# A linear-attention and feed-forward kernel on one core: u loaded to all partitions, fillers on TensorE, a written order for steps 0 to 2

## The chip, the core and the metric

The kernel runs on one core of a Trainium2 chip. A core has five engines that run side by side, each through its own list of instructions in order: TensorE (PE in the profile; PEld is its loading of weights), VectorE (DVE), ScalarE (ACT), GpSimd (POOL) and SyncE (SP), which here issues the loads. Engines wait for each other by semaphores. The metric is the device time of one execution in microseconds, as the median of timed runs. The profile is of one further execution, which has a time of its own.

## What is computed

Two parts follow each other. Per batch and head, with a state of 48 x 48:

```
for t in range(S):                       # B, H, S, D = 4, 8, 768, 48
    cur = einsum('bhd,bhe->bhde', u * k[t], v[t])
    y[t] = einsum('bhd,bhde->bhe', r[t], state + cur)
    state = w * state + einsum('bhd,bhe->bhde', k[t], v[t])
x = y as 3072 tokens x 384
h = x @ w_in                             # 384 -> 2048
out = where(h > 0, h, exp(min(h, 0)) - 1) @ w_out    # 2048 -> 384
```

## The kernel before

The 768 times are cut into 6 blocks of 128 (NCH, index n). In a block there are 4 units, one for each batch b. A unit's attention is done by blocks: r and k are turned by TensorE (`turn_in`, L601, a transpose by the identity), multiplied by powers of w (`decay_r` and `decay_k`, L676 and L684, both through L667 on DVE), multiplied with each other to scores (L741 in block 0), masked, and applied to v (L797). The part of the current token is sum over d of r u k, times v: `current` (L693) makes ru in two multiplications, `current_sum` (L703) the sum. `key_rest` (L708) multiplies k by the reversed powers `rev` for the state, and `added_state` (L888) makes the addition to the state. The outputs of a block, in two parts xh and xl, are the x of the layer.

The layer goes in 16 steps per block (NF, index f), of 128 hidden units each: `hid` (9 matmuls of 128 x 512, L1004), `neg` (two on ACT, L1013 and L1014), `elu` (DVE, L1019), `gh` (ACT, L1025), `gl` (DVE, L1027), `proj` (9 matmuls, L1048). While block 0's layer runs, block 1's units are prepared, and the weights of the layer are loaded and split in two parts. Load j (`Lw:j`, `load_weights`, L200) brings columns of w_in for step j/2 in 4 pieces where j is even, rows of w_out where j is odd, into slot (j+1) mod 6 of `stage`. A load is then widened (`wd:k`, ACT, L550, two loads at once), merged (`ma:k`, DVE, L559) and split: `sp:k`, and the remainder `rs:j` or `rsd:j` (L594, L596), which reads the slot last. So Lw:12 can start only when rsd:6 is done.

All loads go through SP's queue in written order; an issue that waits holds up those behind it. Nothing is moved by a scheduler (`manual_schedule`): each engine's list is the order of the calls. Three lists make it: START (block 0's units and first weights), BOTH (steps 0 and 1) and FIRST and LATER (a pattern for each further step), read by `start`, `first_steps` and `step`. At the beginning, in `prepare`, 7 matmuls on the identity go ahead (`warm`), u is loaded as one row, and `u_by_tokens` (L500) spreads it to 128 partitions by one matmul with a column of ones, copied by ACT.

Of the kernel before, what the change touches and what calls it, by code (L numbers as in the profile page):

```python
# [8 lines left out]
F32 = mybir.dt.float32  # L9
# [42 lines left out]
FIRST = """
Lq rk3 v3 Eq1 hid ns3 A1 T0 rud0 ma sum0 bkA-1 neg df0 elu sp dk0 pa1 brA-1 Y2 gh gl dr0 pb1 r4d xh2 xl2 mbT+1 mrT+1
# [13 lines left out]
class Kernel:  # L67
# [7 lines left out]
    def prepare(self, ctx):  # L75
        nc, tc = self.nc, self.tc
        cp = ctx.enter_context(tc.tile_pool(name="cp", bufs=1))

        self.rev = cp.tile([P, H, DP], F32, tag="rev", name="rev")
        self.state = [cp.tile([P, HP, 2 * D], F32, tag=f"state{b}", name=f"state{b}") for b in range(B)]  # L80
        early = self.rev.rearrange("p h d -> p (h d)")
        w_row = early[0:1, 0:DM]
        nc.sync.dma_start(w_row, self.w.rearrange("(o h) d -> o (h d)", o=1))

        w_col = cp.tile([P, HP], F32, tag="w_col", name="w_col")
        nc.vector.memset(w_col, 1.0)
# [213 lines left out]
    def run(self):  # L300
        self.start()
        self.first_steps()
        for at in range(2, NCH * NF):
            self.step(*divmod(at, NF))
        for f in (NF - 2, NF - 1):
            self.project(NCH - 1, f)
        self.store(NCH - 1)

    def start(self):
# [3 lines left out]
        for b in (2, 3):  # L313
# [59 lines left out]
    def first_steps(self):  # L373

        layer = {
            "hid": lambda f: self.hidden(0, f, self.rest_of(0, f)),
            "neg": lambda f: self.negative(0, f),
            "elu": lambda f: self.elu(0, f),
            "gh": lambda f: self.split_g(0, f, 0),
            "gl": lambda f: self.split_g(0, f, 1),  # L380
            "proj": lambda f: self.project(0, f),
        }
        for op in BOTH.split():
            if ":" in op:
                self.do(op)
            else:
                layer[op[:-1]](int(op[-1]))

    def next_loads(self, b):
        self.raw[1, b] = self.slots[b]  # L390
# [109 lines left out]
    def u_by_tokens(self):  # L500

        ps = self.bank("u")[:, 0:DM]
        self.nc.tensor.matmul(ps, lhsT=self.one, rhs=self.u_row, start=True, stop=True)
        self.nc.scalar.copy(self.u_b.rearrange("p h d -> p (h d)"), ps)

    def inverse_table(self):

# [183 lines left out]
            self.scaled(un["k"], un["pk"], self.qw, by_act)  # L691

    def current(self, n, b, eng=None):  # L693

        nc, wk, un = self.nc, self.wk, self.units.setdefault((n, b), {})
        r_t, k_t, _ = self.raw[n, b]
        un["ru"] = wk.tile([P, H, D], F32, tag="ru", name="ru", bufs=2)
        (eng or nc.gpsimd).tensor_mul(un["ru"], r_t[:, :, 0:D], self.u_b)
        (eng or nc.gpsimd).tensor_mul(un["ru"], un["ru"], k_t[:, :, 0:D])
# [431 lines left out]
```

## Time and profile before

| | us |
|---|---|
| median of 3 timed runs | 505.28 (504.96 to 506.22) |
| the profiled execution | 510.23 |
| its span, first to last instruction | 508.5 |
| PE busy in the span | 494.7 |
| mean granted clock of TensorE in the span | 0.988 |

The profiled execution stands 4.95 us above the median. Of its time 1.7 us lie outside the span. Times in the trace are counted from the span's start. TensorE's clock has two levels, 2.4 GHz and 1.2 GHz; a granted clock of 1.00 is the first, 0.50 the second. A matmul's busy time is modelled, so a busy PE may still be a slow one; the clock tells which.

### The profile page before, as it was taken

The numbers are of one execution on the slowest core, as the hardware profiler recorded it, in microseconds if no ns is written. First come the engines' busy times: TensorE is split into PE (matmuls) and PEld (weight loads), VectorE is DVE, ScalarE is ACT, GpSimd is POOL, SyncE is SP. The second block draws the span as 40 slices with busy tenths as digits, with TensorE's granted clock in tenths as the row PEclk, the third lists the DMA queues.
The fourth block names the chain that finished last, engine by engine and source line by source line (L and its number), as shares of the span: only waits on it lengthen the run. The fifth ranks groups of instructions, "written<-read, shape, count | busy, mean of one in ns | idle before, by whom it ended". The sixth has DMA issues, their size and how long they took to land.

```text
span 508.5 us, 12107 instructions
## 1 busy us (share of the span) xinstructions
PE 494.7 (97%) x5005; PEld 406.5 (80%) x5005; DVE 304.9 (60%) x531; ACT 240.8 (47%) x459; POOL 107.2 (21%) x142
## 2 busy tenths in 40 slices
PE   7999999999999999999999999999999999999995
PEld 6887777887888888887878888888788878899995
DVE  6786988975865666666474674574664443343331
ACT  2276677744454435435534354354354354344442
POOL 7514224333123141321321212211011000000000
PEclk8799999999999999999999999999999999999999
DMA  8869777665256434625613446326243000011001
GB/s 137 232 154 218 165 188 186 139 135 126 58 121 148 109 68 85 147 70 109 131 44 88 110 74 134 98 46 127 66 97 101 18 1 2 8 28 24 6 0 67
DMA packets 108453, 49.11 MB, mean 97 GB/s; under 512 B 89442, under 2 KB 104292, under 8 KB 108388
## 3 DMA queue, kind: packets, MB, share of 16 engines
q1 hardware_dynamic: 96292, 43.52, 38.6%
q10 hardware_dynamic: 12096, 4.72, 3.9%
q8 instruction: 41, 0.67, 0.5%
q14 instruction: 24, 0.20, 0.1%
HBM read 35.12 MB, written 13.11 MB: 95 GB/s over the span
## 4 chain that ended last, share of the span: by engine, by line
PE 89%; DMA 5%; ACT 2%; DVE 1%; SPq 1%; issue 1%; POOL 0%; ACTq 0%; DVEq 0%
PE ps_acc L1048 38%; PE ps_h L1004 36%; PE ps_y L797 4%; PE ps_a L765 3%; DMA r_t<-in_r_dram 2%; DMA stage<-in_moe_w_in_dram 2%; PE ps_a L741 2%; PE ps_y L785 1%; PE ps_y L897 1%; ACT wide L550 1%; DMA stage<-in_moe_w_out_dram 1%; PE ps_y L780 1%; PE ps_rT L607 1%; PE ps_kT L607 1%; PE ps_y L853 1%
## 5 line engine op out<-in xcount | busy, mean ns | idle before, releaser
L1004 PE MATMUL ps_h<-x,wh 128*128 128x512 f32 (+1 forms) x582 | 180.2, 391 | 0.0
L1048 PE MATMUL ps_acc<-g,wh 128*128 128x512 f32 x480 | 165.8, 400 | 1.1 <-issue 1.0
L1019 DVE SCALAR_TENSOR_TENSOR ps_h<-g,ps_h 128x512 f32<-128x512 f32 x96 | 66.7, 694 | 137.1 <-ACT g L1014 137.0
L1004 PEld LDWEIGHTS ps_h<-x,wh 128*128 128x128 f32 x582 | 108.5, 188 | 22.8
L1013 ACT ACTIVATE g<-ps_h 128x512 f32<-128x512 f32 x96 | 57.3, 597 | 135.5 <-PE ps_h L1004 125.5
L1004 PE MATMUL ps_h<-x,wl 128*128 128x512 f32 (+1 forms) x291 | 114.0, 392 | 0.0
L1048 PEld LDWEIGHTS ps_acc<-g,wh 128*128 128x128 f32 x480 | 90.0, 188 | 22.4 <-issue 1.1
L1048 PE MATMUL ps_acc<-g,wl 128*128 128x512 f32 x240 | 93.6, 390 | 0.0
L1027 DVE SCALAR_TENSOR_TENSOR g<-ps_h,g 128x512 fp32r<-128x512 f32 x96 | 66.3, 691 | 40.3 <-ACT g L1025 34.8
L1025 ACT ACTIVATE g<-ps_h 128x512 fp32r<-128x512 f32 x96 | 57.5, 599 | 69.6 <-DVE ps_h L1019 69.5
L1004 PEld LDWEIGHTS ps_h<-x,wl 128*128 128x128 f32 x291 | 54.6, 188 | 12.8
L1014 ACT ACTIVATE g<-g 128x512 f32<-128x512 f32 x96 | 60.7, 632 | 3.1
L815 POOL TENSOR_TENSOR a<-ident,diag 128x512 f32<-128x512 f32 x20 | 20.9, 1043 | 156.9 <-PE ps_y L897 81.8
L1048 PEld LDWEIGHTS ps_acc<-g,wl 128*128 128x128 f32 x240 | 45.1, 188 | 9.9 <-issue 0.9
L1048 PE MATMUL ps_acc<-wh,g 128*128 128x384 f32 x128 | 35.3, 339 | 0.0
L655 POOL TENSOR_TENSOR tb<-rk,qw 128x512 f32<-128x512 f32 x16 | 20.7, 1296 | 67.6 <-DMA rk<-blocks 50.8
L822 DVE COPY_PREDICATED a<-mask,ps_a 128x512 f32<-128x512 int32 x40 | 29.3, 733 | 0.0
L811 ACT ACTIVATE a<-ident,diag 128x128 f32<-128x128 f32 x80 | 25.3, 391 | 0.0
L1048 PEld LDWEIGHTS ps_acc<-wh,g 128*128 128x128 f32 x128 | 23.4, 187 | 1.1 <-issue 0.4
L1048 PE MATMUL ps_acc<-wl,g 128*128 128x384 f32 x64 | 21.6, 337 | 0.0
L922 ACT CAST x<-ps_y 128x256 fp32r<-128x256 f32 (+1 forms) x40 | 10.8, 324 | 22.5 <-DVE state L912 21.0
L570 POOL CAST wh<-stage 128x384 fp32r<-128x384 f32 x16 | 8.6, 534 | 57.1 <-DVE stage L559 57.1
(112 smaller groups left out, 456.2 us busy)
## 6 DMA issues: line engine op xcount, KB each, us to landing
blocks<-tb SPq DMA_DIRECT2D x64, 128.0 KB, 2.3
rk<-blocks SPq DMA_DIRECT2D x16, 512.0 KB, 3.5
stage<-in_moe_w_out_dram SPq DMA_DIRECT2D x16, 383.8 KB, 3.8
stage<-in_moe_w_in_dram SPq DMA_DIRECT2D x64, 95.8 KB, 3.7
out_dram<-stage ACTq DMA_DIRECT2D x80, 48.0 KB, 1.7
r_t<-in_r_dram SPq DMA_DIRECT2D x17, 192.0 KB, 4.5
k_t<-in_k_dram SPq DMA_DIRECT2D x17, 192.0 KB, 5.0
v_t<-in_v_dram SPq DMA_DIRECT2D x17, 192.0 KB, 5.3
```

Of the source, the lines that this page charges most:

```text
L655: (self.nc.gpsimd if i else self.nc.vector).tensor_mul(dst, src, by)
L797: self.nc.tensor.matmul(y[self.pair(a), t : t + P], lhsT=v[:, d : d + Q], rhs=un["a"][i][:, a, :], start=(n == 0 and j != 1 and len(un["py ...
L811: self.nc.scalar.activation(un["a"][i][:, a, :], self.ident, AF.Copy, scale=diag[:, a : a + 1])
L815: self.nc.gpsimd.tensor_mul(un["a"][i], self.ident.unsqueeze(1).to_broadcast([P, HP, P]), diag.unsqueeze(2).to_broadcast([P, HP, P]),)
L822: self.nc.vector.copy_predicated(un["a"][i], self.mask.bitcast(I32).unsqueeze(1).to_broadcast([P, HP, P]), un["pa"][i].rearrange("p (a t) ...
L1004: self.nc.tensor.matmul(ph[:, part], lhsT=a[:, c * P : (c + 1) * P], rhs=x[:, c, part], start=(c == 0 and i == 0), stop=(c == NC - 1 and i ...
L1013: nc.scalar.activation(g, ph, AF.Relu, scale=-1.0)
L1014: nc.scalar.activation(g, g, AF.Exp, scale=-1.0)
L1019: self.nc.vector.scalar_tensor_tensor(ph, g, -1.0, ph, op0=ALU.add, op1=ALU.max)
L1025: nc.scalar.activation(part, g, AF.Copy, scale=W_SCALE)
L1027: nc.vector.scalar_tensor_tensor(part, g, W_SCALE, self.g[n, f][2].bitcast(F32), op0=ALU.mult, op1=ALU.subtract)
L1048: self.nc.tensor.matmul(at, lhsT=lhs, rhs=rhs, start=(f == 0 and i == 0), stop=(f == NF - 1 and i == 2),)
```

## The change

Four things are edited. First, u is loaded by one DMA with its row repeated for all 128 partitions, behind k of unit 0 and ahead of r of unit 1; the matmul, the copy and the small load go. In `current` the product r k is made first and then multiplied by u, so the first product needs no u. Second, fillers: `jk:9` puts 9 transposes of the identity on PE ahead of unit 0's first transpose, `jk:3` puts 3 ahead of unit 1's; nothing reads them. Third, START is in a new order, and BOTH now holds steps 0, 1 and 2 as one written order (the pattern begins with step 3). Fourth, the first unit of block 1 (`nT`, `ndr`, `ndk`, `nru`, `nsum`, `nDp`) is turned and decayed at written places, sooner than the pattern did it.

```diff
 START = """
 Lrk:2 Lv:1 Lrk:3 Lv:2 Lw:0 Lv:3 Lw:2 Lw:1 Lw:4 Lw:3 Lw:5
-pr ub Tr:0 inv ru:0 Tk:0 Tr:1 dr:0 zw Tk:1 dk:0 A:0 dr:1 dk:1 sum:0 Tr:2 A:1 Tk:2 m0:0 m1:0 ru:1 dr:2 m0:1 dk:2 vd:0 PT Tr:3
...
+jk:9 Tr:0 inv pr Tk:0 rua:0 dr:0 dk:0 rub:0 rua:1 sum:0 PT zw rub:1 jk:3 krd:0 Tr:1 Tk:1 dk:1 dr:1 A:0 S:0 Tr:2 Tk:2
...
 BOTH = """
-hid0 neg0 krd:3 S:1 Ln:1 ma:2 elu0 Sd:2 gh0 gl0 hid1 neg1 sp:2 elu1 rsd:4 Lw:10 gh1 S:3 proj0 gl1 rs:3 Lw:9 wd:3
-ma:3 sp:3 rsd:6 rs:5 wd:4
+xh:3 xl:2 xl:3 wdo:1 hid0 rsd:2 krd:3 krd:1 wd:2 neg0 ma:2 mao:1 sp:2 elu0 hid1 krd:2 gh0 spo:1 nT:0 wd:3 rs:1 gl0
+Lw:8 Sd:1 rsd:4 ma:3 neg1 elu1 Lw:7 rs:3 Lw:9 ndr:0 ndk:0 sp:3 proj0 gh1 gl1 hid2 nru:0 rsd:6 neg2 S:3 wd:4 elu2 Lw:12
+ma:4 Lw:10 proj1 gh2 nsum:0 rsd:5 nDp:0 Ln:1 gl2 sp:4 Sd:2 rs:7 rsd:8 Lw:11 wd:5
 """
...
-        self.u_row, self.one = early[DP : DP + 1, 0:DM], ones[DP : DP + 1, :]
-        nc.sync.dma_start(self.u_row, self.u.rearrange("(o h) d -> o (h d)", o=1))
         self.load_rk(0, 0, (1,))
+        nc.sync.dma_start(self.u_b, self.u.partition_broadcast(P))
...
-        for at in range(2, NCH * NF):
+        for at in range(3, NCH * NF):
...
+            "ndr": lambda b: self.now("df", b, self.decay_r),
+            "ndk": lambda b: self.now("df", b, self.decay_k),
...
+    def now(self, name, b, what, *args):
+        self.done.add((name, 1, b))
+        what(1, b, *args)
...
+    def keep_warm(self, times):
+        junk = self.ps.tile([P, T], F32, tag="h", name="junk", bufs=2)
+        for _ in range(times):
+            self.nc.tensor.transpose(junk[:, 0:P], self.ident, self.ident)
...
+    def key_product(self, n, b, eng=None):
+        un = self.units.setdefault((n, b), {})
+        r_t, k_t, _ = self.raw[n, b]
+        un["ru"] = self.wk.tile([P, H, D], F32, tag="ru", name="ru", bufs=2)
+        (eng or self.nc.gpsimd).tensor_mul(un["ru"], r_t[:, :, 0:D], k_t[:, :, 0:D])
```

In the rows of order below, a row is an engine's instruction (or several, x4) with its line, what it writes and what it reads; lines of the changed file are some 9 to 15 higher. PE at the program's start before: r_t_68 and k_t_69 are unit 0's, r_t_71 and k_t_72 unit 1's, `raw` units 2 and 3.

```order
L503 MATMUL ps_u<-rev 128x384
L607 MATMUL ps_rT<-ident,r_t_68 128x128 x4
L607 MATMUL ps_kT<-ident,k_t_69 128x128 x4
L607 MATMUL ps_rT<-ident,r_t_71 128x128 x4
L607 MATMUL ps_kT<-ident,k_t_72 128x128 x4
L741 MATMUL ps_a<-rk 128x128 x8
L607 MATMUL ps_rT<-ident,raw 128x128 x4
```

The same place now:

```order
L513 MATMUL junk<-ident 128x128 x9
L616 MATMUL ps_rT<-ident,r_t_68 128x128 x4
L616 MATMUL ps_kT<-ident,k_t_69 128x128 x4
L538 MATMUL ps_pt<-ident,pwr 128x128 x4
L513 MATMUL junk<-ident 128x128 x3
L616 MATMUL ps_rT<-ident,r_t_71 128x128 x4
L616 MATMUL ps_kT<-ident,k_t_72 128x128 x4
L756 MATMUL ps_a<-rk 128x128 x8
```

The fillers stand ahead of both units' transposes, and the transposes of the powers (ps_pt) have come forward from behind unit 2's.

SP's queue before, from the last load of START's first line on (w_in is even loads, w_out odd ones): the second row is Lw:6, then block 1's unit 0, Lw:7, Lw:8, block 1's unit 1, Lw:10, Lw:9 with Lw:11, and Lw:12.

```order
L215 DMA stage<-in_moe_w_out_dram 128x1535 x2
L212 DMA stage<-in_moe_w_in_dram 32x3x511 x4
L165 DMA r_t_68<-in_r_dram 128x8x48
L165 DMA k_t_69<-in_k_dram 128x8x48
L169 DMA v_t_70<-in_v_dram 128x8x48
L215 DMA stage<-in_moe_w_out_dram 128x1535
L212 DMA stage<-in_moe_w_in_dram 32x3x511 x4
L165 DMA r_t_71<-in_r_dram 128x8x48
L165 DMA k_t_72<-in_k_dram 128x8x48
L169 DMA v_t_73<-in_v_dram 128x8x48
L212 DMA stage<-in_moe_w_in_dram 32x3x511 x4
L215 DMA stage<-in_moe_w_out_dram 128x1535 x2
```

The same place now: block 1's unit 0, Lw:6 and Lw:8, Lw:7 and Lw:9, Lw:12 and Lw:10, block 1's unit 1, Lw:11 with Lw:13.

```order
L214 DMA stage<-in_moe_w_out_dram 128x1535 x2
L164 DMA r_t_68<-in_r_dram 128x8x48
L164 DMA k_t_69<-in_k_dram 128x8x48
L168 DMA v_t_70<-in_v_dram 128x8x48
L211 DMA stage<-in_moe_w_in_dram 32x3x511 x8
L214 DMA stage<-in_moe_w_out_dram 128x1535 x2
L211 DMA stage<-in_moe_w_in_dram 32x3x511 x8
L164 DMA r_t_71<-in_r_dram 128x8x48
L164 DMA k_t_72<-in_k_dram 128x8x48
L168 DMA v_t_73<-in_v_dram 128x8x48
L214 DMA stage<-in_moe_w_out_dram 128x1535 x2
```

Block 1's unit 0 has moved ahead of Lw:6, and Lw:12 ahead of Lw:10.

DVE before, from ma:3 to the first mask of block 1's unit 0 (wl_131 is rsd:6, wl_133 is rsd:8; ps_h is elu):

```order
L559 SCALAR_TENSOR_TENSOR stage<-stage,wide 128x768
L596 SCALAR_TENSOR_TENSOR wl_131<-stage,wh_130 128x384
L698 TENSOR_TENSOR ru<-r_t_68,u_b 128x384
L699 TENSOR_TENSOR ru<-ru,k_t_69 128x384
L559 SCALAR_TENSOR_TENSOR stage<-stage,wide 128x768
L706 TENSOR_REDUCE diag<-ru 128x8
L667 TENSOR_TENSOR rk<-ps_rT,pw 128x512
L667 TENSOR_TENSOR rk<-ps_kT,qw 128x512
L1019 SCALAR_TENSOR_TENSOR ps_h<-g,ps_h 128x512
```

Now, from ma:3 to rsd:6 and the elu behind it:

```order
L568 SCALAR_TENSOR_TENSOR stage<-stage,wide 128x768
L1034 SCALAR_TENSOR_TENSOR ps_h<-g,ps_h 128x512
L676 TENSOR_TENSOR rk<-ps_rT,pw 128x512
L676 TENSOR_TENSOR rk<-ps_kT,qw 128x512
L1042 SCALAR_TENSOR_TENSOR g_651<-ps_h,g_649 128x512
L712 TENSOR_TENSOR ru<-r_t_68,k_t_69 128x384
L716 TENSOR_TENSOR ru<-ru,u_b 128x384
L605 SCALAR_TENSOR_TENSOR wl_131<-stage,wh_130 128x384
L1034 SCALAR_TENSOR_TENSOR ps_h<-g,ps_h 128x512
```

The two decays of block 1's unit 0 (rk) have moved ahead of an elu, and rsd:6 from right behind ma:3 to six instructions further on.

## Rows read from the trace of the kernel before

**Rows 1.** The page, parts 1 and 2: busy us by engine; granted clock.
```profile
PE 494.7 (97%) x5005; PEld 406.5 (80%) x5005; DVE 304.9 (60%) x531; ACT 240.8 (47%) x459; POOL 107.2 (21%) x142
...
PEclk8799999999999999999999999999999999999999
```

**Rows 2.** Windows: us; busy us (count) by engine; PEclk; DMA; GB/s.
```profile
5.00:8.50 3.50, 2.34 (x12) 1.40 (x13) 2.96 (x8) 3.33 (x4) 2.05 (x7) 0.96 1.37 188
...
8.50:18.80 10.30, 10.19 (x72) 8.37 (x75) 6.53 (x11) 0.58 (x1) 5.65 (x7) 0.52 1.05 215
...
24.00:28.00 4.00, 3.79 (x125) 3.53 (x122) 3.46 (x8) 2.64 (x6) 0.83 (x1) 1.00 0.23 91
...
29.00:44.50 15.50, 15.49 (x177) 12.54 (x167) 11.72 (x20) 11.29 (x20) 4.06 (x6) 1.00 0.97 199
...
44.50:45.60 1.10, 0.01 (x2) 0.01 (x2) 1.10 (x3) 0.00 (x0) 1.10 (x2) 1.00 1.01 373
...
502.60:506.50 3.90, 0.01 (x1) 0.00 (x0) 0.56 (x1) 0.03 (x1) 0.00 (x0) 1.00 0.57 199
...
506.50:508.50 2.00, 0.00 (x0) 0.00 (x0) 0.00 (x0) 0.00 (x0) 0.00 (x0) 0.52 0.04 13
```

**Rows 3.** Timeline of PE to 21 us: start, length, work [idle before].
```profile
5.03 0.88 PE L503 MATMUL ps_u<-rev 1*128 1x384 f32 x2
...
7.05 0.63 PE L607 MATMUL ps_kT<-ident,k_t 128*128 128x128 f32 x4 [0.55 <-DMA k_t<-in_k_dram]
...
8.26 1.09 PE L607 MATMUL ps_rT<-ident,r_t 128*128 128x128 f32 x4 [0.58 <-DMA r_t<-in_r_dram]
...
20.02 0.66 PE L607 MATMUL ps_kT<-ident,raw 128*128 128x128 f32 x4
```

**Rows 4.** Timeline of SP's queue, 20 to 42 us.
```profile
20.49 0.90 SPq L215 DMA_DIRECT2D stage<-in_moe_w_out_dram  x2
...
27.82 1.75 SPq L212 DMA_DIRECT2D stage<-in_moe_w_in_dram  x4
...
39.45 2.50 SPq L212 DMA_DIRECT2D stage<-in_moe_w_in_dram  x4
```

**Rows 5.** The page, part 6: issues, KB each, us to landing.
```profile
stage<-in_moe_w_in_dram SPq DMA_DIRECT2D x64, 95.8 KB, 3.7
...
blocks<-tb SPq DMA_DIRECT2D x64, 128.0 KB, 2.3
```

**Rows 6.** SP's waits, 20 to 50 us: total, times, longest.
```profile
SPq L212 <- DVE wl L596: 7.5, 2, 6.4
```

**Rows 7.** Timeline, step 3: from a weight load's landing to PE.
```profile
47.21 1.09 ACT L550 ACTIVATE wide<-stage 128x768 f16<-128x768 bf16 x1 [0.44 <-DMA stage<-in_moe_w_out_dram]
...
51.20 0.72 DVE L822 COPY_PREDICATED a<-mask,ps_a 128x512 f32<-128x512 int32 x1
...
51.97 0.18 PEld L780 LDWEIGHTS ps_y<-rk,state 48*32 48x32 f32 x14 [0.39 <-DVE a L822]
```

**Rows 8.** Groups by line, 27 to 52 us: busy, mean ns.
```profile
L1019 DVE SCALAR_TENSOR_TENSOR ps_h<-g,ps_h 128x512 f32<-128x512 f32 x4 | 2.8, 694 | 3.1 <-ACT g L1014 3.1
...
L1027 DVE SCALAR_TENSOR_TENSOR g<-ps_h,g 128x512 fp32r<-128x512 f32 x4 | 2.8, 692 | 0.9 <-ACT g L1025 0.9
...
L1014 ACT ACTIVATE g<-g 128x512 f32<-128x512 f32 x4 | 2.5, 632 | 0.1
...
L596 DVE SCALAR_TENSOR_TENSOR wl<-stage,wh 128x384 fp32r<-128x384 f32 x5 | 2.8, 558 | 0.6 <-ACT wh L572 0.6
```

**Rows 9.** Timeline of DVE, 38 to 45 us.
```profile
38.95 0.96 DVE L559 SCALAR_TENSOR_TENSOR stage<-stage,wide 128x768 int32<-128x768 int32 x1 [0.94 <-ACT wide L550]
...
41.02 1.40 DVE L698 TENSOR_TENSOR ru<-r_t,u_b 128x384 f32<-128x384 f32 x1
...
42.45 0.56 DVE L699 TENSOR_TENSOR ru<-ru,k_t 128x384 f32<-128x384 f32 x1
...
44.26 0.68 DVE L667 TENSOR_TENSOR rk<-ps_rT,pw 128x512 f32<-128x512 f32 x1
```

More of the change, by code (lines that the diff above doesn't have):

```diff
@@ L42 @@
 Lrk:2 Lv:1 Lrk:3 Lv:2 Lw:0 Lv:3 Lw:2 Lw:1 Lw:4 Lw:3 Lw:5
-pr ub Tr:0 inv ru:0 Tk:0 Tr:1 dr:0 zw Tk:1 dk:0 A:0 dr:1 dk:1 sum:0 Tr:2 A:1 Tk:2 m0:0 m1:0 ru:1 dr:2 m0:1 dk:2 vd:0 PT Tr:3
-m1:1 Y:0 sum:1 Tk:3 xh:0 ru:2 krd:0 A:2 dr:3 sum:2 vd:1 ru:3 wd:0 dk:3 xl:0 Y:1 m1:2 m0:2 ma:0 A:3 xh:1 sum:3 vd:2 m1:3 sp:0
-m0:3 wdi:1 vd:3 Y:2 xl:1 mai:1 xh:2 krd:1 wdo:1 Y:3 spi:1 xh:3 rsd:0 Lw:6 mao:1 spo:1 S:0 Ln:0 xl:2 wd:2 xl:3 H:0 rsd:1 Lw:7
-rsd:2 Lw:8 krd:2
+jk:9 Tr:0 inv pr Tk:0 rua:0 dr:0 dk:0 rub:0 rua:1 sum:0 PT zw rub:1 jk:3 krd:0 Tr:1 Tk:1 dk:1 dr:1 A:0 S:0 Tr:2 Tk:2
+A:1 m0:0 m1:0 dr:2 vd:0 Tr:3 dk:2 m0:1 m1:1 A:2 wd:0 Tk:3 ru:2 sum:2 sum:1 vd:2 dr:3 vd:1 dk:3 ru:3 Y:0 m0:2 A:3 m1:2
+ma:0 Y:2 sum:3 m0:3 Y:1 m1:3 sp:0 wdi:1 xh:0 xh:2 xl:0 xh:1 vd:3 mai:1 Ln:0 rsd:0 xl:1 spi:1 Lw:6 Y:3 H:0
 """
 BOTH = """
-hid0 neg0 krd:3 S:1 Ln:1 ma:2 elu0 Sd:2 gh0 gl0 hid1 neg1 sp:2 elu1 rsd:4 Lw:10 gh1 S:3 proj0 gl1 rs:3 Lw:9 wd:3
-ma:3 sp:3 rsd:6 rs:5 wd:4
+xh:3 xl:2 xl:3 wdo:1 hid0 rsd:2 krd:3 krd:1 wd:2 neg0 ma:2 mao:1 sp:2 elu0 hid1 krd:2 gh0 spo:1 nT:0 wd:3 rs:1 gl0
+Lw:8 Sd:1 rsd:4 ma:3 neg1 elu1 Lw:7 rs:3 Lw:9 ndr:0 ndk:0 sp:3 proj0 gh1 gl1 hid2 nru:0 rsd:6 neg2 S:3 wd:4 elu2 Lw:12
+ma:4 Lw:10 proj1 gh2 nsum:0 rsd:5 nDp:0 Ln:1 gl2 sp:4 Sd:2 rs:7 rsd:8 Lw:11 wd:5
 """
@@ L254, in run_general @@
     def run_general(self):
-        self.u_by_tokens()
         self.reverse_powers()
@@ L318, in start @@
         ops = {
-            "ub": lambda b: self.u_by_tokens(),
+            "jk": lambda b: self.keep_warm(b),
+            "rua": lambda b: self.key_product(0, b),
+            "rub": lambda b: self.times_u(0, b),
+            "nT": lambda b: self.now("T", b, self.turn_in),
+            "nru": lambda b: self.now("rud", b, self.current, dve),
+            "nsum": lambda b: self.now("sum", b, self.current_sum),
+            "ndr": lambda b: self.now("df", b, self.decay_r),
+            "ndk": lambda b: self.now("df", b, self.decay_k),
+            "nDp": lambda b: self.now("Dp", b, self.diag_scores, 0),
             "inv": lambda b: self.inverse_table(),
@@ L498, in warm @@
                 self.nc.tensor.matmul(junk, lhsT=self.ident, rhs=self.ident, start=True, stop=True)
[L500 to L504, printed above, removed]
+    def keep_warm(self, times):
+        junk = self.ps.tile([P, T], F32, tag="h", name="junk", bufs=2)
+        for _ in range(times):
+            self.nc.tensor.transpose(junk[:, 0:P], self.ident, self.ident)
     def inverse_table(self):
@@ L693, in current, with times_u @@
     def current(self, n, b, eng=None):
[L695 to L699, printed above, removed]
+        self.key_product(n, b, eng)
+        self.times_u(n, b, eng)
         if self.general:
             self.current_sum(n, b)
+    def key_product(self, n, b, eng=None):
[3 more added lines that the diff above has]
+        (eng or self.nc.gpsimd).tensor_mul(un["ru"], r_t[:, :, 0:D], k_t[:, :, 0:D])
+    def times_u(self, n, b, eng=None):
+        ru = self.units[n, b]["ru"]
+        (eng or self.nc.gpsimd).tensor_mul(ru, ru, self.u_b)
     def current_sum(self, n, b):
```

## Prediction

> **What bounds the kernel now.** I read the page first: PE is busy for 494.7 of 508.5 us, so the end is PE's, and what a change can give is PE's waiting and the time in which its clock is low [rows 1]. The row of the granted clock, in 40 slices of 12.7 us, is full from the third slice on; only the first two show less. So I went to the windows. From 5 to 8.5 us PE is busy for 2.34 of 3.50 us. From 8.5 to 18.8 us it is busy for 10.19 of 10.30 us at a mean granted clock of 0.52, that is at 1.2 GHz nearly throughout; before and after it is at 2.4 GHz [rows 2]. The work of those 10.19 us would take about 5.1 us at the full clock: the most that can be had there. That the low clock is what costs is seen on one instruction group: four transposes take 1.09 us at 8.26 and 0.66 us at 20.02 [rows 3]. What PE did before the fall: a matmul of one row (u), and the transposes of unit 0, with two waits for loads of 0.55 and 0.58 us (k of unit 0 at 7.05, r of unit 1 at 8.26) [rows 3].
>
> Then I asked what PE would meet if it came earlier. From 29 to 44.5 us it is busy for 15.49 of 15.50 us, so no row shows it waiting for weights there; but the DMA share is 0.97 at 199 GB/s [rows 2]: the loads are as full as PE, only just ahead of it. In step 3 the order turns: ACT's widening at 47.21 waited for a weight load, and from its start a chain of ACT and DVE goes to the mask at 51.20 and to PE's scores by state at 51.97 [rows 7]. That is 51.97 - 47.21 = 4.76 us from a landed load to PE. This place decides the sum.
>
> **The change part by part.**
>
> *u by a load.* Removed: PE's 0.88 us at 5.03 [rows 3], ACT's copy, a small DMA. Added: a 192 KB DMA ahead of r of unit 1 and everything behind. No row shows a load with repeated rows. Bounds from rows: loads of the same size land 8.26 - 7.05 = 1.2 us apart at the start [rows 3]; at the best rate of a row, 373 GB/s [rows 2], 0.197 MB take 0.53 us. Less than that has no reason, since the bytes are written all the same. I take 0.8, between them, since its runs of 1536 bytes are eight times those of r. The Trainium skill (DMA: Bandwidth & Descriptors, Specifications) gives 512 bytes as the least piece at full rate; by it the lower end would hold and the sum be 0.3 us better. No row shows it for this load.
>
> *Fillers.* Twelve transposes at 0.66 / 4 = 0.165 us [rows 3]: 1.5 us for the nine, 0.5 us for the three. PE is free from about 5.0, the nine end at 6.5; Tr:0 then ends at 7.2 and Tk:0, whose load lands at 7.0, follows. The three stand before r of unit 1, which now lands near 8.26 + 0.8 = 9.1. Both lie in waits, cost nothing on the path, and at the low clock would take up to 1.6 us more, half of it still covered. With them, PE is busy for about 3.3 of the 3.5 us up to 8.5 where it was 2.34. I take it that the clock then stays at 2.4 GHz. PE arrives at step 1 some 4 to 5 us sooner (5.1, less what the loads of units 2 and 3 hold back, which come 0.8 us later).
>
> *The order of steps 0 to 2: what of that lead is left.* The loads are next to be late, and I follow them in four terms.
> (a) Lw:6. Before, it was issued at 27.82 [rows 4] after SP had waited 6.4 us for a remainder on DVE [rows 6], and the DMA engines idled: 91 GB/s from 24 to 28 us, at a share of 0.23 [rows 2]. What moved in those 4 us, 0.364 MB, was the end of START's first line; at 199 GB/s [rows 2] it takes 1.8 us, so the queue was through at about 25.8. Now block 1's unit 0 (576 KB) and Lw:6 (383 KB) follow at once, with u 192 KB more: 1151 KB, 1.18 MB, which at 199 GB/s [rows 2] take 5.9 us, at 373 GB/s 3.2. I take the former, as it is the mean of the stretch that holds the same kinds of loads, and 0.3 for the last piece: Lw:6 has landed at about 32.0 (29.0 to 33, the latter with 1.2 for u and the slower issue).
> (b) From there to rsd:6, on which Lw:12 waits: the widening 1.09 [rows 7]; two passes on ACT for neg1 at 0.63 each, 1.26, longer than the merge on DVE, 0.96, beside it; elu1 0.69; two decays at 0.68, 1.36; gl1 0.69; two products at 0.56, 1.12; rsd:6 0.56 [rows 8, 9]. The sum is 6.8. A product took 1.40 where POOL ran beside it [rows 9], so up to 7.6. rsd:6 ends at 32.0 + 6.8 = 38.8.
> (c) Lw:12 and, behind it, Lw:10: eight pieces. Four take SP 1.75 to 2.50 us [rows 4], so the eighth is issued 3.5 to 5.0 us on, at 42.3 or later; pieces of this kind land 3.7 us after issue in the median, and the shortest median of the page is 2.3 [rows 5]. I take 3.0, between them, the queue being empty in front of these: 45.3 (from 42.3 + 2.3 = 44.6 to 43.8 + 3.7 = 47.5).
> (d) wd:5 then starts at 45.3, and 4.76 later, at about 50.0, PE goes on; before it was 51.97.
> Gain: 2.0 us. Ends: all late, 33 + 7.6 + 5.0 + 3.7 + 4.76 = 54.1, a loss of 2.1; all early, 29.0 + 6.8 + 3.5 + 2.3 + 4.76 = 46.4, a gain of 5.6, which the lead of PE itself limits to about 4.5. In front of this place PE must wait: its lead of 4 to 5 us turns into 2.0, so 2 to 3 us are spent there, beside 0.4 before [rows 7].
>
> *Block 1's first unit decayed sooner.* PE's wait of 1.1 us from 44.5 to 45.6 [rows 2] goes, since the two decays stand ahead of what kept DVE; but it lies ahead of the place of (d) and adds nothing beyond it. DVE's six instructions in front of rsd:6 are the price, in (b).
>
> *The rest* (START's new order, key_rest and the state sooner, r k before u): the same instructions, hidden behind loads as before; 0 on the path.
>
> From step 3 on both kernels have the same order, loads and PE alike shifted by the gain, so it stays to the end. Against the profiled execution: 510.23 - 2.0 = 508.2, a span of 506.5. Against the median: 505.28 - 2.0 = 503.3.
>
> **The rivals.**
>
> *1. The loads come sooner.* The best rate of rows 2 rather than the mean. Then PE's lead of 4 to 5 us stays: 505.28 - 4.5 = 500.8. For it: after 24 us the DMA engines have room. Against: the share of 0.97 from 29 us on.
>
> *2. The gain is given back whole.* Lw:10 lands no sooner than 46.5, because it stands behind Lw:12. Then (d) is 51.3 and the gain 0.7: 504.6. For it: the ends of (b) and (c).
>
> *3. The clock falls a second time, in the wait that the change makes.* Place: PE in front of the scores by state, step 3. By the sum it stands still for 2 to 4 us. Rows show two cases: a wait of 1.1 us left the clock at 1.00; behind the last matmul it was 1.00 for 3.9 us and then 0.52 [rows 2]. A wait like the former changes nothing, one like the latter brings this rival; the forecast's wait lies between the two, nearer to the latter. The price: if the low stretch is as long as the first, PE's work of about 10 us takes 5.1 us more; if a third as long, 1.7. I take 4.0, nearer to the former, since the first low stretch went on although PE was busy for 10.19 of 10.30 us in it [rows 2]: 503.3 + 4.0 = 507.3. The Trainium skill (TensorE: Matmul & The Clock Gate, HAM oscillation — how this bites in real kernels) says that waits for loads between bursts of matmuls put the clock low again. The trace agrees at the kernel's end, but at 8.5 us the clock fell with no wait above 0.6 us, so the rule is not the whole of it.
>
> *4. The timed runs have no low stretch, or fillers do not prevent it.* The profiled execution is 4.95 us longer than the median, about as much as the low stretch costs. If the timed runs lack it, the lead is there already, and the change only brings the wait: 3 us of it, 508.3. If the clock falls all the same, the change has the u load (0.8) and nothing else: 506.1. For it: that likeness in size. Against: loads, waits and PE's list are the same in timed runs, and a low stretch that came and went among them would spread them by more than the 1.3 us from 504.96 to 506.22.
>
> **How the numbers follow.** The chances: forecast 0.44 (501.8 to 504.2), rival 1 0.10, rival 2 0.15, rival 3 0.17 (505.0 to 508.4), rival 4 0.14 (506.1 to 508.3). About 0.3% (1.5 us) is what a measurement of this kernel can tell from no change. Faster by more than that (below 503.76): 0.36 of the forecast's and all of rival 1, together 0.46. Within: 0.08 of the forecast's, rival 2's 0.15, 0.05 of rival 3 and 0.02 of rival 4: 0.30. Slower (above 506.80): what is left of rivals 3 and 4, 0.24. The likeliest is the forecast, 503.3. The range is 500.8 to 507.4; it leaves out the lower half of rival 1 and the upper parts of rivals 3 and 4, some 0.18.
>
> **What would show it.** Right: a granted clock of 1.00 through 8.5 to 18.8 us; PE at step 1's first hid about 4 us sooner; then, in step 3, PE's longest wait of the program, 2 to 4 us, in front of the scores by state, ended by DVE's mask, behind ACT's wd:5, behind a w_in load; and from there on every row some 2 us sooner. Wrong: a low clock that starts at about 11 us (rival 4) or at about 50 us (rival 3), no wait in step 3 (rival 1), or a profiled time that falls while the median does not (rival 4).

## The result, and the profile after

The changed kernel takes 509.06 us in the median (508.81 to 510.19), where the kernel before takes 505.12 beside it: a ratio of 1.0078 with a 95% interval from 1.0057 to 1.0100. It is slower by 3.9 us; the forecast was 2.0 us faster. Its profiled execution, however, is shorter than that of before: 509.18 us at a span of 507.4, against 510.23 at 508.5. Both statements hold, and the difference between them is the first thing to explain.

The page of the changed kernel, with the granted clock in 40 slices:

```profile
span 507.4 us, 12116 instructions
PE 491.9 (97%) x5015; PEld 404.3 (80%) x5015; DVE 304.6 (60%) x533; ACT 239.7 (47%) x456; POOL 107.2 (21%) x142
PEclk9999999999999999999999999999999999999999
```

Its windows, as in [rows 2]: stretch and its length, busy time of PE, PEld, DVE, ACT and POOL with instructions, granted clock, DMA share, GB/s:

```profile
5.00:8.50 3.50, 3.47 (x24) 3.48 (x24) 2.60 (x8) 1.64 (x3) 1.79 (x7) 1.00 0.81 166
8.50:18.80 10.30, 8.34 (x143) 6.80 (x144) 8.68 (x16) 2.53 (x4) 6.48 (x7) 1.00 0.89 180
...
29.00:44.50 15.50, 13.69 (x155) 10.00 (x155) 12.81 (x23) 8.88 (x16) 5.65 (x7) 1.00 0.56 153
```

The low stretch of 8.5 to 18.8 us is gone: PE does 143 instructions there where it did 72. But it now waits, 2.0 us there and 1.8 us from 29 to 44.5, where before it was busy throughout. The DMA share from 29 to 44.5 us has fallen from 0.97 to 0.56: the loads are not short of bandwidth, they are not issued. What PE waits for, and the chain behind it:

PE's timeline of the changed kernel (start, length, line, operation, idle time before and what ended it), the first part of hid1 and the scores by state of step 3:

```profile
28.27 0.63 PE L1019 MATMUL ps_h<-x,wh 128*128 128x512 f32 x2
...
31.36 0.63 PE L616 MATMUL ps_kT<-ident,k_t 128*128 128x128 f32 x4 [0.41 <-DMA k_t<-in_k_dram]
...
38.23 0.50 PE L1063 MATMUL ps_acc<-g,wh 128*128 128x512 f32 x1 [0.97 <-ACT g L1040]
...
51.48 0.45 PE L795 MATMUL ps_y<-rk,state 48*32 48x128 f32 x14 [1.70 <-DVE a L837]
```

ACT's timeline, the widenings of Lw:6 (with Lw:5) and of Lw:10 (with Lw:9):

```profile
34.63 1.09 ACT L559 ACTIVATE wide<-stage 128x768 f16<-128x768 bf16 x1 [3.36 <-DMA stage<-in_moe_w_in_dram]
...
46.71 1.09 ACT L559 ACTIVATE wide<-stage 128x768 f16<-128x768 bf16 x1 [3.80 <-DMA stage<-in_moe_w_in_dram]
```

SP's timeline. The row at 23.48 ends START's first line (Lw:3, Lw:5), that at 29.28 is Lw:6 and Lw:8, that at 33.64 Lw:7 and Lw:9, that at 40.93 Lw:12 and then Lw:10:

```profile
3.19 0.81 SPq L109 DMA_DIRECT2D u_b<-in_u_dram  x1
...
5.14 2.89 SPq L168 DMA_DIRECT2D v_t<-in_v_dram  x1
9.03 0.37 SPq L164 DMA_DIRECT2D raw<-in_r_dram  x1
...
23.48 0.90 SPq L214 DMA_DIRECT2D stage<-in_moe_w_out_dram  x2
...
29.28 4.19 SPq L211 DMA_DIRECT2D stage<-in_moe_w_in_dram  x8
33.64 0.83 SPq L214 DMA_DIRECT2D stage<-in_moe_w_out_dram  x2
40.93 3.64 SPq L211 DMA_DIRECT2D stage<-in_moe_w_in_dram  x8
```

And SP's waits from 27 to 50 us (in total, times, longest):

```profile
SPq L211 <- DVE wl L605: 6.4, 1, 6.4
```

From 34.5 to 40.9 us SP stands before the first piece of Lw:12, which waits for rsd:6 on DVE. Lw:10 stands behind it with nothing to wait for (its slot was free after rsd:4), and Lw:10 is what ACT, DVE and PE wait for in step 3. It is the place that the prediction named; the gain there is 51.97 - 51.48 = 0.5 us against the profiled execution of before, not 2.0.

**The two groups of before.** Beside the twelve kernels below, e1 to e12, the kernel before ran 114 times. Its times fall in two groups with nothing between 507.43 and 508.24: 76 executions with a median of 505.7 and mean granted clocks of 0.993 to 1.000, and 38 with a median of 509.1, of which 31 have a mean clock of 0.983 to 0.993. The profiled execution (510.23, clock 0.988) belongs to the second, the runs that were timed for the prediction to the first. So the prediction started from a profile of the rarer kind, and most executions of before are not of that kind. A low stretch is seen in that one profile; the mean clock of the 31 fits one, and why the other 7 are long (0.997 to 0.999) is not shown. The groups are 3.4 us apart. Differences below are to the median of the first group among the executions of before that ran beside the kernel in question. That median itself lies between 505.1 and 506.5, so a difference of half a microsecond between kernels that did not run side by side settles little; the changed kernel (four executions), e1 to e4, e5 to e8, e9 to e11 and e12 are five such sets.

### The profile page after: what moved, and what is told of

It reads as the page before. It is cut to its first block, busy times and chain, and to the rows that moved or that the text cites. A ratio compares the mean times of both kernels' runs of the same rounds, so it can differ in the third digit from the quotient of the medians.

```text
span 507.4 us, 12116 instructions
## 1 busy us (share of the span) xinstructions
PE 491.9 (97%) x5015; PEld 404.3 (80%) x5015; DVE 304.6 (60%) x533; ACT 239.7 (47%) x456; POOL 107.2 (21%) x142
## 4 chain that ended last, share of the span: by engine, by line
PE 86%; DMA 5%; SPq 4%; ACT 2%; DVE 1%; issue 1%; POOL 0%; ACTq 0%; DVEq 0%; POOLq 0%
PE ps_acc L1063 38%; PE ps_h L1019 36%; PE ps_a L780 3%; PE ps_y L812 3%; SPq L211 2%; DMA stage<-in_moe_w_out_dram 2%; DMA r_t<-in_r_dram 1%; PE ps_y L800 1%; ACT wide L559 1%; DMA stage<-in_moe_w_in_dram 1%; PE ps_y L912 1%; PE ps_y L795 1%; PE ps_a L756 1%; PE junk L508 1%; SPq L164 1%
## 5 line engine op out<-in xcount | busy, mean ns | idle before, releaser
L559 ACT ACTIVATE wide<-stage 128x768 f16<-128x768 bf16 (+1 forms) x18 | 17.9, 994 | 16.6 <-DMA stage<-in_moe_w_in_dram 14.5
```

Of the source, the lines that this page charges most:

```text
L559: self.nc.scalar.activation(top.rearrange("p s (f t) -> p s f t", t=2)[..., 1], self.place(self.late, k, DEEP, i).bitcast(BF16)[..., 2], A ...
```

## The experiments

All figures in one place, in us. "Scores" is the time in the profile at which PE goes on with the scores by state of step 3; from there to the end of the span it is 454.5 to 456.5 us in all kernels, so this one time says, to 2 us, what the first steps cost in the profiled execution.

| kernel | median | to before | profiled: scores, span |
|---|---|---|---|
| before (median of its first group; low stretch in the profile) | 505.1 to 506.5, by set | 0 | 51.97, 508.5 |
| changed | 509.06 | +3.9 | 51.48, 507.4 |
| e1 before + fillers | 505.57 | -0.1 | 48.09, 503.6 |
| e2 before + u by a load | 510.77 | +5.1 | 53.87, 509.2 |
| e7 before + fillers + u by a load | 506.06 | +0.5 | 48.43, 504.1 |
| e3 changed, u by a matmul | 507.73 | +2.0 | 50.88, 506.9 |
| e4 changed, no fillers | 509.41 | +3.7 | 51.03, 506.8 |
| e5 changed, Lw:10 ahead of Lw:12 | 505.66 | +0.1 | 48.32, 503.6 |
| e6 changed, Lw:6 ahead of Ln:0 | 508.33 | +2.7 | 50.75, 506.5 |
| e8 changed, e3, e5 and e6 together | 504.52 | -1.1 | 47.81, 502.6 |
| e9 as e5, no fillers | 506.21 | +0.7 | 49.06, 504.2 |
| e10 as e5, u by a matmul | 504.45 | -1.1 | 46.93, 501.4 |
| e11 as e8, block 1's unit 0 turned later | 503.32 | -2.2 | 48.03, 502.6 |
| e12 as e1, block 1's unit 0 decayed sooner | 505.75 | -0.75 | 49.93, 505.6 |

### Is the low stretch in the timed runs? (e1)

```diff
-pr ub Tr:0 inv ru:0 Tk:0 Tr:1 dr:0 zw
+jk:9 pr ub Tr:0 inv ru:0 Tk:0 jk:3 Tr:1 dr:0 zw
```

> The kernel before with the twelve fillers alone (nine ahead of u's matmul, three ahead of the transposes of unit 1); u by a matmul, the old order. Theory A: the timed runs of before have the full clock already and only its profiled execution had the low stretch; then the fillers change nothing in the median (505.1, within 0.7), while the profiled span falls from 508.5 to about 503.5 at a granted clock near 1.00. Theory B: the low stretch is in every execution of before, and the change wins it back but loses more by order and loads; then the fillers alone give 505.1 - 4.5 = 500.6. Theory C: the fillers do not keep the clock; 505.1 to 506.7, and the profile shows the low stretch again.

505.57 us: theory A. Nine of twelve executions lie from 504.3 to 506.3, as before's first group does; three lie at 508.3 to 508.9. The profiled span falls by 4.9 us, the median not at all. That three of twelve are long, where 12 of the 33 executions of before beside it are, does not show that the fillers make long executions rarer here; two of the three have mean clocks of 0.997 and 0.999. The window of the former low stretch:

```profile
8.50:18.80 10.30, 10.29 (x190) 8.62 (x188) 10.11 (x18) 2.27 (x4) 9.81 (x11) 1.00 1.04 212
...
29.00:44.50 15.50, 14.24 (x106) 11.02 (x105) 10.93 (x18) 9.68 (x16) 5.58 (x7) 1.00 1.06 220
```

This profile, not that of before, is what the changed kernel must be compared with. In it PE goes on with the scores at 48.09:

```profile
41.10 1.16 PE L747 MATMUL ps_a<-rk 48*128 48x128 f32 x16 [1.10 <-DVE rk L673]
...
48.09 0.45 PE L786 MATMUL ps_y<-rk,state 48*32 48x128 f32 x14 [0.78 <-DVE a L828]
```

51.48 - 48.09 = 3.4 us: the loss.

### The load of u (e2, e7, e3)

e2 is the kernel before with u's load in place of `ub`; e7 is the same with the fillers; e3 is the changed kernel with the matmul again.

```diff
-        self.u_row, self.one = early[DP : DP + 1, 0:DM], ones[DP : DP + 1, :]
-        nc.sync.dma_start(self.u_row, self.u.rearrange("(o h) d -> o (h d)", o=1))
         self.load_rk(0, 0, (1,))
+        nc.sync.dma_start(self.u_b, self.u.partition_broadcast(P))
```

> The kernel before with u by a load with repeated rows alone; no fillers, the old order. In the profile of after, SP began the loads of unit 2 at 9.03 us where before began them at 7.37, 1.66 us later. Theory A (full clock in timed runs, so that the loads bound the first steps): 505.1 + 1.7 = 506.8. Theory B (low stretch in all runs, PE being late there, so that the loads have room): 505.1 to 505.9. My prediction's price for the load, 0.8, would give 505.9.

510.77 us, above all that was expected; one execution of ten took 507.89. The load takes away more than a matmul: without it PE stands idle ahead of unit 0 (0.62 us) and of unit 1 (2.07 us). PE's timeline of e2:

```profile
5.51 1.09 PE L598 MATMUL ps_rT<-ident,r_t 128*128 128x128 f32 x4 [0.62 <-DMA r_t<-in_r_dram]
...
9.52 1.08 PE L598 MATMUL ps_rT<-ident,r_t 128*128 128x128 f32 x4 [2.07 <-POOL ru L689]
10.63 1.09 PE L598 MATMUL ps_kT<-ident,k_t 128*128 128x128 f32 x4
...
18.48 1.06 PE L598 MATMUL ps_rT<-ident,raw 128*128 128x128 f32 x4
...
21.97 0.66 PE L598 MATMUL ps_kT<-ident,raw 128*128 128x128 f32 x4
```

Four transposes take 1.06 to 1.09 us until 18.5 and 0.66 at 22: PE is at 1.2 GHz until then. By the times, before is long in one execution of three, e2 in nine of ten (seen in the clock of one profile each). With the fillers:

> The kernel before with fillers and u by a load, the old order. The fillers alone gave 505.6 (9 of 12 executions between 504.3 and 506.3). If the load of u costs what SP loses by it (1.66 us): 507.2. If the prediction's 0.8: 506.4. If the old order hides it: 505.6. If order and load only cost together: 505.6 here, and 507.7 to 509.1 was their sum.

506.06 us (ten of twelve below 506.8, two at 508.4 and 509.5). So the fillers are worth 4.7 us where u comes by a load in the old order, and nothing can be seen of them where it does not (e1). The load itself, with the fillers in (e7 against e1), costs 0.5 to 0.6, within what such a comparison can tell from nothing.

> The changed kernel with u by PE's matmul again; fillers and new order kept. If the load of u costs what SP lost (1.66 us): 509.1 - 1.7 = 507.4. If it costs the 0.8 of the prediction: 508.3. If its cost is hidden: 509.1. In the profile Lw:6 should land by as much sooner than at 34.5 us, and the scores by state go on by as much sooner than at 51.5.

507.73 us: 1.3 to 1.9 us less than the changed kernel (by medians and by the differences to before). In the profile the widening of Lw:6 is only 0.7 us sooner (33.92) and the scores 0.6 (50.88), so that the expectation of 1.66 there was too high. With Lw:10 first the load costs 1.2 (e5 against e10). So what SP loses by it, 1.66 us, is nearly paid in the new order and at most a third of it in the old one. In SP's rows above, the issue of unit 0's v, the third load behind u's, takes 2.89 us, where before it took 1.20, and unit 2's r is issued at 9.03 instead of at 7.37. All profiles show this: with u by a load (seven of them) v's issue takes 2.30 to 2.96 us and unit 2's r is issued at 8.51 to 9.12; with the matmul (seven) it is 0.81 to 1.20 and 6.89 to 7.37. The rows of before:

```profile
5.17 1.20 SPq L169 DMA_DIRECT2D v_t<-in_v_dram  x1
7.37 0.37 SPq L165 DMA_DIRECT2D raw<-in_r_dram  x1
```

### The fillers in the new order (e4)

Without `jk:9` and `jk:3`.

> The changed kernel without its twelve fillers; load of u and new order kept. Theory A (timed runs have the full clock without fillers): 509.1, within 0.7. Theory B (without fillers the clock is low from 8.5 to 18.8 us in every execution): 509.1 + up to 5 us, less what the waits of the first steps swallow (about 10 us of PE's time to 60 us is waiting in after): 510 to 513. A profile with the low stretch and a median without it would speak for A.

509.41 us, so theory A again, and more than that: the profiled execution of e4 does have a low stretch, and it is no slower (508.64 against 509.18).

```profile
8.50:18.80 10.30, 8.96 (x94) 7.38 (x96) 6.38 (x11) 1.60 (x3) 5.74 (x6) 0.67 0.91 186
...
29.00:44.50 15.50, 15.50 (x174) 11.91 (x173) 14.76 (x27) 10.00 (x17) 6.13 (x8) 1.00 0.60 160
```

The clock is at a mean of 0.67 from 8.5 to 18.8 us and PE then has no wait from 29 to 44.5 us; with fillers it waits there 1.8 us. Either way it meets the scores at 51.0 to 51.5, here after a wait:

```profile
51.03 0.45 PE L795 MATMUL ps_y<-rk,state 48*32 48x128 f32 x14 [1.82 <-DVE a L837]
```

A faster PE buys next to nothing here (0.35 us by the medians, 0.2 the other way by the differences to before), in front of a place that a load sets.

### The order of the loads (e5, e6, e8)

e5 exchanges two names in BOTH:

```diff
-... rsd:6 neg2 S:3 wd:4 elu2 Lw:12
-ma:4 Lw:10 proj1 ...
+... rsd:6 neg2 S:3 wd:4 elu2 Lw:10
+ma:4 Lw:12 proj1 ...
```

> The changed kernel with Lw:10 and Lw:12 exchanged (Lw:10, which step 3's hidden layer needs first, is issued first). Theory Q1: Lw:12 ahead of Lw:10 sets step 3. Then ACT's widening moves from 46.7 us to about 44.9 (four pieces take SP 1.8 us), PE's wait of 1.7 us ahead of the scores by state goes, and the median is 509.1 - 1.7 = 507.4. Theory Q2: the order of these two only shifts the wait to the next weights (Lw:12 is then late by as much): 508.5 to 509.1.

505.66 us: theory Q1, by twice as much as it said. One exchange gives back 3.4 us, since Lw:10 needs no wait at all: SP issues it at 34.75, 8 us sooner, not only the 1.8 us of four issues. The row of SP, then those of ACT's widening and PE's scores:

```profile
34.75 6.85 SPq L211 DMA_DIRECT2D stage<-in_moe_w_in_dram  x8
```

```profile
41.77 1.08 ACT L559 ACTIVATE wide<-stage 128x768 f16<-128x768 bf16 x1
```

```profile
48.32 0.45 PE L795 MATMUL ps_y<-rk,state 48*32 48x128 f32 x16
```

The widening is 4.9 us sooner and waits for no load; PE's scores are 3.2 us sooner, with no wait in front. The span falls by 3.8 us, to that of e1.

e6 moves Ln:0 (block 1's unit 0, 576 KB) behind Lw:6:

```diff
-... mai:1 Ln:0 rsd:0 xl:1 spi:1 Lw:6 Y:3 H:0
+... mai:1 rsd:0 xl:1 spi:1 Lw:6 Ln:0 Y:3 H:0
```

> The changed kernel with Ln:0 (r, k, v of block 1's unit 0, 576 KB) behind Lw:6 instead of ahead of it, as the kernel before has it. Theory R1: what the new order loses at the full clock begins with these 576 KB ahead of Lw:6; at the 255 to 265 GB/s that the profiles show there they are 2.2 us. Then the widening of Lw:6 moves from 34.6 to about 32.4 us, the waits of 1.0 and 0.4 behind it go, and the median is 509.1 - 1.4 to 2.2, 507.3. Theory R2: PE then waits for k of block 1's unit 0, whose transposes the new order has sooner (0.41 us of waiting at 31.4 in after, 2 us more here), and nothing is won: 509.1.

508.33 us, between the two: 0.7 less than the changed kernel by the medians, 1.2 by the differences to before, 0.9 by the spans. Lw:6 is widened 3.5 us sooner (31.17), but PE's transposes of block 1's unit 0 then wait longer, and Lw:10 still stands behind Lw:12. DVE's merge behind the widening is only 0.9 us sooner (34.86; 35.75 in the changed kernel), because the copies of the state ahead of it wait for PE. SP's issue of Lw:12 is 1.0 us sooner (39.91). e6's ACT, DVE and PE:

```profile
31.17 1.07 ACT L559 ACTIVATE wide<-stage 128x768 f16<-128x768 bf16 x1
```

```profile
33.61 0.74 DVE L929 COPY state<-ps_st 48x192 f32<-48x192 f32 x2 [1.61 <-PE ps_st L912]
...
34.86 0.95 DVE L568 SCALAR_TENSOR_TENSOR stage<-stage,wide 128x768 int32<-128x768 int32 x1
```

```profile
31.24 0.63 PE L616 MATMUL ps_rT<-ident,r_t 128*128 128x128 f32 x4 [1.12 <-DMA r_t<-in_r_dram]
32.43 0.63 PE L616 MATMUL ps_kT<-ident,k_t 128*128 128x128 f32 x4 [0.57 <-DMA k_t<-in_k_dram]
...
50.75 0.45 PE L795 MATMUL ps_y<-rk,state 48*32 48x128 f32 x14 [1.58 <-DVE a L837]
```

> The changed kernel with u by PE's matmul, Lw:6 ahead of Ln:0, and Lw:10 ahead of Lw:12; fillers and the rest of the new order kept. If these three are what the change loses: 505.6 as with the fillers alone, and, since the block's first unit is decayed sooner (the fillers alone leave a wait of 1.1 us for that at 41 us), down to 504.5. If the rest of the new order loses too: 506.5 to 507.5.

504.52 us, the lower of what was expected. Which of the three does it, e10 shows below.

### What the mended order is worth, and what it is bound by (e9, e10, e11)

> The changed kernel with Lw:10 ahead of Lw:12 and without the fillers. So far: fillers were worth 4.7 us where the old order has u by a load (510.8 without, 506.1 with them), and 0.3 in the changed kernel (509.4 without, 509.1 with them). Theory S: in the changed kernel SP's wait in front of Lw:12 sets the time of step 3 whatever PE's clock, so fillers can give nothing; with that wait gone (505.7 with fillers) they count again, and without them it is 508.5 to 510.2. Theory T: the new order is proof against the low clock by itself: 505.7 to 506.2.

506.21 us: theory S falls. In its profiled execution (506.06 us) the clock is low as in e4, and the time without fillers is 0.5 to 0.6 us longer than e5's, not 3 to 4.5. The low stretch and the scores of e9:

```profile
8.50:18.80 10.30, 9.04 (x92) 7.57 (x94) 6.25 (x11) 1.97 (x3) 5.48 (x6) 0.67 0.96 193
```

```profile
49.06 0.45 PE L795 MATMUL ps_y<-rk,state 48*32 48x128 f32 x16
```

PE has no listed wait between 11 and 60 us in it, where e5 has three that sum to 1.8 us; most of what a slow PE loses, a quick one would have waited. So the new order with Lw:10 first is nearly proof against the low clock by itself, and the fillers are worth about 0.5 us in it, which these runs hardly tell from nothing.

> The changed kernel with Lw:10 ahead of Lw:12 and u by PE's matmul; fillers, and Ln:0 ahead of Lw:6, kept. The load of u cost 0.5 in the old order (506.1 against 505.6) and 1.4 in the changed one (509.1 against 507.7): 505.7 - 0.5 to 1.4 = 504.3 to 505.2. If Lw:6 ahead of Ln:0 was what made 504.5 of the version with all three mended, this is 505.2 or more; if it gave nothing, 504.5 or less.

504.45 us (ratio 0.9953, interval 0.9924 to 0.9982). It has Ln:0 ahead of Lw:6 and is as good as e8 (both 1.1 us below before), so of e8's three parts the exchange of Lw:6 gave nothing that can be seen; Lw:10 first and u by a matmul are enough. e10's scores, 1.4 us sooner than e5's:

```profile
46.93 0.45 PE L804 MATMUL ps_y<-rk,state 48*32 48x128 f32 x16
```

e11 is e8 with the transposes and decays of block 1's unit 0 behind the projection of step 0:

```diff
-... spo:1 nT:0 wd:3 ... Lw:9 ndr:0 ndk:0 sp:3 proj0 gh1
+... spo:1 wd:3 ... Lw:9 sp:3 proj0 nT:0 ndr:0 ndk:0 gh1
```

> The version with all three mended (504.5), and the transposes and decays of block 1's unit 0 behind the projection of step 0 instead of ahead of it: PE waited 1.00 and 0.58 us for r and k there, since these loads now stand behind Lw:6. If that wait is on the path: 504.5 - 1.6 = 502.9. If it only moves PE's wait to a later weight load: 504.5. If DVE's decays come too late for the products in front of rsd:6 and so for Lw:12: 505 or more.

503.32 us, 1.2 less than e8 where 1.6 was the wait, and 1.1 less than e10, which ran beside it. That the wait was on the path is what this suggests; the profile does not show it. In e11's profiled execution (504.43 us, the second longest of the twelve) both waits are gone, but PE goes on with the scores at 48.03, 0.2 us later than in e8, since it stands 1.1 us longer at another place, for nothing that the profile names (0.54 us there in e8):

```profile
24.68 0.49 PE L877 MATMUL ps_y<-ident,vd 128*32 128x128 f32 x9 [1.66 <-issue]
```

The ratio to before is 0.9926 with an interval from 0.9896 to 0.9955, in which before's long executions count (11 of the 29 beside it; the highest of e11's twelve is 506.31); against the others it is 2.2 us. It is faster than both kernels.

### Block 1's first unit decayed sooner, alone (e12)

e1 with `nT:0` behind `proj0` and the decay ahead of `rsd:6`.

> The kernel before with the fillers (505.6), and block 1's unit 0 turned behind the projection of step 0 and decayed on DVE ahead of rsd:6, as one part of the change alone. In the fillers' profile PE waited 1.10 us at 41.1 for DVE's decay of this unit and 0.78 us ahead of the scores by state. The prediction's reading: the first wait goes, but the weights set step 3, so the second grows by as much: 505.6. The rival: DVE, not the weights, is late there, since its decays stood behind the products and a merge, and PE's path has no other wait to give it back: 504.5 to 504.8. If DVE's decays make rsd:6 and so a weight load later: 506 or more.

505.75 us. The wait of 1.10 us at 41.1 is gone and that in front of the scores has grown from 0.78 to 1.25, as the prediction read it; but this profiled execution, the slowest of its twelve, has a wait of 2.03 us for a weight, where the other profiles show at most 0.42 there:

```profile
32.81 0.47 PE L1060 MATMUL ps_acc<-g,wh 128*128 128x512 f32 x1 [2.03 <-POOL wl L606]
...
49.93 0.45 PE L792 MATMUL ps_y<-rk,state 48*32 48x128 f32 x14 [1.25 <-DVE a L834]
```

So its waits cannot tell what the part does in the median. By the median it gives nothing, by the difference to before beside it 0.6; the ratios of e12 and e1 (0.9968, from 0.9946 to 0.9989; 0.9987, from 0.9959 to 1.0014) overlap. Whether it gives something stays open.

## Why the prediction was wrong

**The base.** The step that failed is the last one of the sum, "Against the median: 505.28 - 2.0 = 503.3", and 4.95 of the 5.8 us between 503.3 and 509.06 are its. The sum was made against a profiled execution with a low stretch and carried over to a median of executions without one. Against the profiled execution it said 508.2, and 509.18 came: 1.0 us off. The fillers' gain, the source of the whole forecast, was in the median already: with the fillers alone the profiled span falls by 4.9 us and the median stays within 0.1 us of before's first group (e1). The text had seen the likeness (4.95 us between profile and median, about what the stretch costs) and gave it to rival 4, with 0.14 shared between two cases. Its argument against was that a stretch that comes and goes would spread the runs by more than 1.3 us. It does, from 504.0 to 511.7 in 114 runs; three runs of one group could not show it. At the odds since seen, 76 of 114, three in a row from the first group come up in 30 of 100.

**Rivals 4 and 2** are what happened, together. Rival 4 by its first half: 508.3 was its time, 509.06 the measured one. Its price, a wait of 3 us, stands against scores that come 3.4 us later (48.09 to 51.48). Its sign was named as well: a profiled time that falls while the median does not. Rival 2 is what the profile shows: Lw:10 no sooner than 46.5 (its widening waits until 46.71), PE at 51.3 (51.48), a gain of 0.7 (0.5). Its time, 504.6, failed by the base alone. The chances took the two as excluding each other.

**The fillers.** That they cost nothing is borne out by e1's median, and that the clock stays up by the profile (1.00 from 8.5 to 18.8 us). The nine were put at 1.5 us and take 1.19 to 2.15 in the ten profiles that have them, 2.06 in the changed kernel; the three take 0.49. hid1 began 4.0 us sooner (28.27 above); the row of before:

```profile
32.27 0.73 PE L1004 MATMUL ps_h<-x,wh 128*128 128x512 f32 x2
```

The Trainium skill (TensorE: Matmul & The Clock Gate, HAM oscillation — how this bites in real kernels) has the clock fall by waits for loads between bursts of matmuls. e2 agrees in part: with waits of 0.62 and 2.07 us (the second put down to POOL) nine of ten executions are long, but its profile has the low level at 5.51 already, behind the wait of 0.62. e4 and e9, which have neither u's matmul nor fillers, have it there too (four transposes in 1.09 us at 5.46 and in 1.08 at 5.37). The kernel's end, which the prediction counts as agreeing, is no wait for a load, and no matmul follows it.

**u by a load** was put at 0.8 us (0.53 to 1.2), as a term that moves the loads; in the sum of (a) it stands as 192 KB at 199 GB/s, 1.0 us. SP lost 1.66 by it, and the time rose by 0.5 (old order), 1.2 (mended) and 1.3 to 1.9 (changed). The upper bound came from the landing times of k and r, the lower from the best rate; what was left out is that an issue on SP behind it, that of unit 0's v, takes 1.7 us longer. What the taking away of u's matmul does to PE's idle time was not priced, since the fillers come with it; alone (e2, +5.1 us) it is the dearest edit that was run.

**(a)** Lw:6 at 32.0 (29 to 33): its widening began at 34.63, outside the range. The term took the queue to be through with the first line at about 25.8 plus u's load. But the last row of that line (Lw:3, Lw:5) stands at 23.48 where [rows 4] has 20.49, 3.0 us later, of which 1.66 are what SP lost at the start. Block 1's unit 0 then holds SP to 29.17, most of it in the issue of its v (3.18 us from 25.99), and Lw:6's first piece follows at 29.28, where before had it at 27.82. In before the loads had caught up with a slow PE (91 GB/s from 24 to 28 us [rows 2]); here they are still under way, at 265 GB/s from 24 to 29 us:

```profile
24.00:29.00 5.00, 4.59 (x74) 4.07 (x67) 4.68 (x10) 3.84 (x8) 0.00 (x0) 1.00 1.01 265
```

**(b)** 6.8 us from Lw:6's landing to rsd:6: 34.63 to 40.93 (SP's next issue) is 6.3. **(c)** 6.5 from there to the landing of Lw:10: 40.93 to 46.71 is 5.8. **(d)** 4.76 to PE: 46.71 to 51.48 is 4.77. So links (b) to (d) were sized to within 0.7 us each, and the sum missed by 1.5 because (a) missed by 2.6. That (b) hangs on Lw:6 alone is not so: in e6 Lw:6 is widened 3.5 us sooner and SP's issue behind rsd:6 comes only 1.0 sooner, since DVE's merge then waits for work of PE. The wait in front of the scores was put at 2 to 4 us and is 1.70, since some of PE's lead had already gone into smaller waits (0.97, 0.42 and 0.41 us, and 2.0 us from 8.5 to 18.8).

What the chain was not asked is whether it must be so long: Lw:10 was taken as bound to stand behind Lw:12, and the 6 us that SP stands in between were a term of the sum and not a suspect. Rival 2 had the fact ("because it stands behind Lw:12") and, for the profile, the price; it did not ask whether the order could be otherwise. Against e1 the loss is 3.4 us, and e5's exchange gives the whole of it back.

**The decays sooner**: the wait of 1.1 us goes and another grows; the prediction's zero is neither shown wrong nor shown right by e12.

**From step 3 on nothing changes**: right, 454.5 to 456.5 us in fourteen profiles.

## What to carry to other kernels

Before a profile's waste is counted as a gain, see that the timed runs have it: where the profiled time and the median differ by about the price of the waste, they probably do not, and a handful of timed runs that agree does not settle it. In a queue that issues in written order, go through the entries behind each one that waits and ask which are ready already: two names exchanged gave back all that the change had lost. A change that quickened the engine in front of a place that a load set was worth at most 0.4 us here until the load moved (e4), and with the load moved a slow PE still cost only about 0.5 (e9).

## What the runs showed of the hardware

One list of instructions, with the same loads, ran in two ways: of 114 executions of before, 76 took 504.0 to 507.4 us and 38 took 508.2 to 511.7. Of the 38, 31 have a mean granted clock of 0.983 to 0.993; 7 have 0.997 or more, and what made them long is open. The one profile of before, of an execution of the long kind, has PE at 1.2 GHz for some 10 us. Twelve transposes that nothing reads turned one kind into the other where u came by a load: all ten executions of e2 are at 507.9 us or above, ten of twelve of e7 below 506.8.

A load that repeats one row for all 128 partitions made an issue behind it on the same queue longer: 2.30 to 2.96 us for unit 0's v in seven profiles with it, 0.81 to 1.20 in seven without.

The granted clock of a stretch does not always show the level. In e2's profile it is recorded as 1.00 where PE does 54 instructions in 10.3 us and four transposes take 1.06 to 1.12 us:

```profile
8.50:18.80 10.30, 9.26 (x54) 7.81 (x55) 5.36 (x9) 0.08 (x1) 6.68 (x7) 1.00 1.05 211
...
44.50:52.00 7.50, 6.24 (x31) 4.44 (x30) 5.14 (x9) 4.92 (x10) 4.07 (x5) 0.77 1.08 285
```

In this trace the length of an instruction that recurs tells it more surely than the record. The second row is a second fall in the same execution, some 2 us after a wait of 1.09 us that ended at 46.5. In before, behind a wait of the same length that ended at 45.6 [rows 2], the clock stayed at 1.00 to 51.4. It is rival 3's event, though not in the changed kernel.
